# Attention and gated feed-forward on one core: long load runs, half-height projection tiles, ACT weight casts and an order from a list scheduler in the kernel

## The chip, the core and the metric

One NeuronCore of a Trainium2 chip. The metric is the device time of one execution in microseconds (us); "span" is the part of it that the trace shows, some 2 us less. PE is the matmul engine, DVE the vector engine, ACT the scalar engine, POOL the general one, SP the one that only issues transfers. In the traces of this case an engine that meets a wait lets nothing pass that stands behind it in its own order (ACT stood 4.3 us before a cast while an eviction was ready); the case turns on that.

## The reference, cut to what matters

```python
# q, k, v: (4, 4, 1088, 32) f32; S1, S2: (8, 32); w_gate, w_val: (128, 1536); w_out: (1536, 128)
a = einsum('rd,bhsd->bhsr', S1, x); b = einsum('rd,bhsd->bhsr', S2, x)   # for x = q and x = k
phi = outer(a, b).reshape(..., 64)
kv = einsum('bhsf,bhsd->bhfd', phi(k), v);  z = phi(k).sum(axis=2)
x = (phi(q) @ kv) / (phi(q) @ z + 1e-6)          # heads joined: (4352, 128)
out = (relu(x @ w_gate) * (x @ w_val)) @ w_out   # (4352, 128) f32
```

The attention part of a batch is small and serial; the feed-forward part is large and regular: nine chunks (eight of 512 tokens, one of 256) of 12 slots, each slot with a gate, a value and an output matmul on PE, a relu on ACT and a multiply on DVE.

## The kernel before

Loads go out in many pieces (k and q of a batch: six transfers each, in runs of 1 KB and 128 B), weights are cast to fp16 on the way in by POOL's transfers, and q, k come in two buffers that rotate.

```python
def load_kq(src, b, name, engs):
    dst = inp.tile([128, NBLK, D], FP32, name=name)          # bufs=2
    for h in range(H):
        engs[h % len(engs)].dma_start(
            out=dst[h * D:(h + 1) * D, 0:32].rearrange("t (g c) d -> t g (c d)", g=4),
            in_=src[b, h, 0:SM, :].rearrange("(g t c) d -> t g (c d)", g=4, t=32))
    ...
nc.gpsimd.dma_start(out=wg_sb, in_=moe_w_gate...)            # f32 -> f16 in the transfer
```

The projection contracts over all 128 rows (4 heads x 32) with a block-diagonal S, into 32-column tiles; the sums z are made by a 128x32 matmul after each pair of key-value matmuls:

```python
nc.tensor.matmul(ps[32*g:32*g+32, s*n:s*n+m], s_bd[:, s], kT[b][:, c_cols(g, c0, ...)], ...)
...
for p in range(2):
    nc.tensor.matmul(ps[:, p*64:(p+1)*64]..., st["kp", b, c][:, p*128:(p+1)*128], v4[b][:, 2*p:2*p+2, c], ...)
nc.tensor.matmul(ps[32*j:32*j+32, 128:160], ab[:, 0, o]..., ab[:, 1, o]..., ...)     # z
```

The order is written as a table of slots and then left to the compiler's scheduler (`MANUAL = False`). A chunk's output leaves in one transfer of 256 KB.

## Time and profile before

| | before |
|---|---|
| time, median of the runs | 152.24 us |
| span of the profiled run | 149.9 us |
| first gate matmul | 33.21 us |
| first gate matmul to last output eviction | 112.34 us |
| last output eviction to the end | 4.35 us |

The last three rows cut the span into start, steady stretch and tail. The start is read from the first g_ps record of PE, the end of the stretch from the end of ACT's last o_sb record. The lines themselves are in the prediction below.

### The profile page before, as it was taken

The page shows a single profiled execution, that of the slowest core. Times are in us where ns is not written, and L with a number is a line of the kernel's source. Part 1 is how long each engine was busy: PE and PEld are TensorE (multiplying, and loading weights), DVE is VectorE, ACT ScalarE, POOL GpSimd, SP SyncE. Part 2 cuts the span into 40 slices and gives each one's busy share as a digit, 9 for nine tenths or more (in the row PEclk, how much of TensorE's full clock was granted, in tenths as well). Part 3 has the DMA queues.
Part 4 walks back from the last instruction along what each step waited for, and adds up shares of the span by engine and source line. Part 5 has one row for each costly group of instructions (what it writes and reads, how often), then busy time and mean ns, then how long its engine had stood idle before and what let it go on. Part 6 is the DMA issues. An engine that isn't in the chain of part 4 may idle for free.

```text
span 149.9 us, 2886 instructions
## 1 busy us (share of the span) xinstructions
PE 120.5 (80%) x1038; PEld 61.7 (41%) x1038; DVE 100.2 (67%) x213; ACT 82.1 (55%) x146; POOL 51.5 (34%) x75
## 2 busy tenths in 40 slices
PE   0035966269999998799999879999998899999950
PEld 0014645144463443355544335554543353444620
DVE  4133754905968688698798685867788386889840
ACT  3000000057756557696467469855658785998940
POOL 7500981722820045575001763620176034000000
PEclk9999999758999999999999999999999999999996
DMA  4999999930000070005201000100010010010101
GB/s 80 201 221 200 134 214 205 185 79 2 4 0 0 4 210 0 2 0 171 63 0 70 2 4 0 70 0 4 0 70 0 4 56 16 0 70 7 69 1 37
DMA packets 13535, 9.20 MB, mean 61 GB/s; under 512 B 5840, under 2 KB 12240, under 8 KB 13520
## 3 DMA queue, kind: packets, MB, share of 16 engines
q1 hardware_dynamic: 8032, 6.62, 17.4%
q0 software_dynamic: 5040, 2.29, 13.1%
q10 hardware_dynamic: 448, 0.10, 0.4%
q8 instruction: 8, 0.13, 0.3%
q14 instruction: 7, 0.06, 0.1%
HBM read 9.08 MB, written 2.23 MB: 75 GB/s over the span
## 4 chain that ended last, share of the span: by engine, by line
PE 63%; POOL 9%; DVE 8%; DMA 6%; issue 4%; ACT 3%; SPq 2%; POOLq 1%; DVEq 0%; ACTq 0%
PE g_ps L375 14%; PE v_ps L379 13%; PE ot_ps L393 13%; POOL qp L217 7%; DMA k<-in_k_dram 6%; PE ps_a L285 6%; PE kv_ps L242 5%; DVE ht L386 4%; PE ps_a L337 3%; PE ps_a L201 3%; PE kv_ps L237 3%; POOL a L319 2%; PE ps_a L358 2%; ACT g_sb L377 2%; PE ps_a L407 1%
## 5 line engine op out<-in xcount | busy, mean ns | idle before, releaser
L386 DVE TENSOR_TENSOR ht<-g_sb,v_ps 128x512 f16<-128x512 f16 (+1 forms) x108 | 68.9, 652 | 25.2 <-ACT g_sb L377 15.5
L377 ACT ACTIVATE g_sb<-g_ps 128x512 f16<-128x512 f32 (+1 forms) x108 | 60.6, 576 | 28.9 <-PE g_ps L375 23.7
L379 PE MATMUL v_ps<-xT,wv_sb 128*128 128x512 f16 (+1 forms) x108 | 40.0, 371 | 0.4
L375 PE MATMUL g_ps<-xT,wg_sb 128*128 128x512 f16 (+1 forms) x108 | 39.9, 374 | 0.1
L393 PE MATMUL ot_ps<-ht,wo_sb 128*128 128x512 f16 (+1 forms) x108 | 38.5, 368 | 0.2 <-DVE ht L386 0.2
L217 POOL TENSOR_TENSOR kp<-kab 128x512 f16<-128x512 f32 (+1 forms) x18 | 17.2, 976 | 22.9 <-DVE kab L212 19.2
L343 ACT COPY qpt<-ps_a 128x1024 f16<-128x1024 f16 (+1 forms) x9 | 8.7, 963 | 27.9 <-PE ps_a L337 27.9
L217 POOL TENSOR_TENSOR qp<-a,qab 128x512 f16<-128x512 f32 (+2 forms) x18 | 18.3, 1037 | 0.5
L201 PE MATMUL ps_a<-kT,s_bd 128*32 128x128 f32 x128 | 7.2, 314 | 12.0 <-DVE s_bd L158 8.2
L337 PE MATMUL ps_a<-ident,qp 128*128 128x128 f16 (+1 forms) x72 | 9.6, 238 | 8.4 <-POOL qp L217 8.4
L302 POOL TENSOR_TENSOR bw<-qab 128x128 f32<-128x128 f32 (+1 forms) x8 | 3.6, 454 | 37.1 <-DVE qab L295 37.1
L379 PEld LDWEIGHTS <-wv_sb 128*128 128x128 f16 x108 | 10.6, 98 | 9.6 <-issue 3.4
L375 PEld LDWEIGHTS <-wg_sb 128*128 128x128 f16 x108 | 10.6, 98 | 8.6 <-issue 2.1
L393 PEld LDWEIGHTS <-wo_sb 128*128 128x128 f16 x108 | 10.2, 97 | 7.8 <-issue 1.7
L337 PEld LDWEIGHTS <-qp 128*128 128x128 f16 (+1 forms) x72 | 5.8, 107 | 17.2 <-POOL qp L217 13.5
L285 PE MATMUL ps_a<-qT,s_bd 128*32 128x128 f32 x128 | 9.8, 314 | 0.9 <-DVE qT L188 0.9
L201 PEld LDWEIGHTS ps_a<-kT,s_bd 128*32 128x32 f32 x128 | 3.8, 120 | 15.0 <-DVE s_bd L158 8.2
L242 PE MATMUL kv_ps<-kab 128*32 128x32 f32 x72 | 9.6, 218 | 0.0
L181 DVE STREAM_TRANSPOSE kT<-k 128x384 f32<-128x384 f32 (+1 forms) x12 | 6.3, 536 | 4.3 <-DMA k<-in_k_dram 4.3
L237 PE MATMUL kv_ps<-v,kp 128*128 128x64 f16 x72 | 8.8, 204 | 0.2 <-DVE kp L217 0.2
L237 PEld LDWEIGHTS <-kp 128*128 128x128 f16 x72 | 6.2, 101 | 5.9 <-DVE kp L217 0.3
L285 PEld LDWEIGHTS ps_a<-qT,s_bd 128*32 128x32 f32 x128 | 5.5, 121 | 5.6 <-issue 1.9
(63 smaller groups left out, 98.9 us busy)
## 6 DMA issues: line engine op xcount, KB each, us to landing
k<-in_k_dram SPq DMA_DIRECT2D x16, 128.0 KB
q<-in_q_dram SPq DMA_DIRECT2D x16, 128.0 KB
out_dram<-o_sb SPq DMA_DIRECT2D x8, 256.0 KB
v<-in_v_dram POOLq DMA_DIRECT2D x4, 256.0 KB, 6.3
wg_sb<-in_moe_w_gate_dram POOLq DMA_DIRECT2D x1, 384.0 KB, 7.7
wv_sb<-in_moe_w_val_dram POOLq DMA_DIRECT2D x1, 384.0 KB, 9.7
wo_sb<-in_moe_w_out_dram POOLq DMA_DIRECT2D x1, 384.0 KB, 14.1
k<-in_k_dram SPq DMA_DIRECT2D x8, 16.0 KB
```

Of the source, the lines that this page charges most:

```text
L201: nc.tensor.matmul(ps[32 * g:32 * g + 32, s * n:s * n + m], s_bd[:, s], kT[b][:, c_cols(g, c0, min(c1, NC))], start=True, stop=True)
L217: eng.tensor_tensor(out=dst.rearrange("p c (h i j) -> p (c h) i j", h=H, i=R), in0=a.rearrange("p c h i -> p (c h) i")[:, :, :, None].to_b ...
L237: nc.tensor.matmul(ps[:, p * 64:(p + 1) * 64].rearrange("p (h d) -> p h d", h=2), st["kp", b, c][:, p * 128:(p + 1) * 128], v4[b][:, 2 * p ...
L242: nc.tensor.matmul(ps[32 * j:32 * j + 32, 128:160], ab[:, 0, o].rearrange("p h r -> p (h r)"), ab[:, 1, o].rearrange("p h r -> p (h r)"), ...
L285: nc.tensor.matmul(ps[32 * g:32 * g + 32, s * 128:(s + 1) * 128], s_bd[:, s] if s < 2 else w_s[b], qT[b][:, c_cols(g, 4 * i, 4 * i + 4)], ...
L337: nc.tensor.transpose(st["qpt", key][:, p, c * n:(c + 1) * n], st["qp", key, c][0:n, p * 128:(p + 1) * 128], ident16[0:n, 0:n])
L343: nc.scalar.copy(out=t[:, :, 0:4 * n], in_=st["qpt", key][:, :, 0:4 * n])
L375: nc.tensor.matmul(g_ps[:, :cs], wg_sb[:, j], xT[:, c0:c0 + cs], start=True, stop=True)
L377: nc.scalar.activation(out=g_sb[:, :cs], in_=g_ps[:, :cs], func=ACTF.Relu)
L379: nc.tensor.matmul(v_ps[:, :cs], wv_sb[:, j], xT[:, c0:c0 + cs], start=True, stop=True)
L386: nc.vector.tensor_tensor(out=st["ht", i][:, j, :cs], in0=g_sb[:, :cs], in1=v_ps[:, :cs], op=ALU.mult)
L393: nc.tensor.matmul(st["ot", i][:, :cs], wo_sb[:, j], st["ht", i][:, j, :cs], start=(j == 0), stop=(j == NJ - 1))
```

## The change

Its intent: let k arrive first and in long runs, so that the feed-forward part starts early; halve the PE time of the projections with 64-row tiles, two of them one above the other, each pair writing its own PSUM bank; take z out from between the key-value matmuls; keep the casting of weights off the transfers; and fix the order of every engine by a list scheduler that runs while the kernel is built, with a cost per step and a table of the times at which loads land. The core of the diff:

```diff
-MANUAL = False
+MANUAL = True
+LAND = {"s": 4.8, "k": (5.0, 12.0, 15.0, 20.0), "q": (7.0, 13.0, 16.0, 21.0), "v": 8.0, "w": (11.0, 13.0, 15.0)}
...
+    k4 = [big.tile([128, NB * D], FP32, name=f"k4_{b}") for b in range(B)]
+    def load_kq(dst, src, b, after=None):
+        behind(after, nc.sync.dma_start(out=dst[b], in_=src[b].rearrange("h (t c) d -> (h t) (c d)", t=32)))
...
+        for rp in range(2):
+            for g in range(4):
+                nc.tensor.matmul(st["ps", key][rp][32 * g:32 * g + 32, lo:lo + 32 * n],
+                                 s_bd[64 * rp:64 * rp + 64].rearrange("p h r x -> p (h r x)"),
+                                 xt[64 * rp:64 * rp + 64, cols(g, c0, c0 + n)], start=True, stop=True)
...
-            nc.sync.dma_start(out=out[...].rearrange("(p c) m -> p c m", p=128)[:, 4 * hf:4 * hf + 4], in_=o)
+            for g0 in (0, 2):
+                ...
+                d = bass.AP(d.tensor, d.offset, [[w * DM, 2], d.ap[0], [1, 4 * DM]])
+                nc.sync.dma_start(out=d, in_=o[32 * g0:32 * g0 + 64].rearrange("p c m -> p (c m)"))
...
+    def cast_w(i):
+        nc.scalar.copy(out=(wg_sb, wv_sb, wo_sb)[i], in_=w_in[i])
...
+    order = run()
+    for _, s in order:
+        s[4](*s[5])
+        if s[4] == k_transpose and s[5] == (0, 1):
+            for i in range(2):
+                load_w(i, st["last"])
+        if s[4] == q_transpose and s[5][1] == 1 and s[5][0] + 1 < B:
+            load_kq(k4, k, s[5][0] + 1, st["last"])
+            if s[5][0] == 0:
+                load_w(2, None)
+            load_kq(q4, q, s[5][0] + 1)
```

## The prediction

> **What bounds the kernel now.** I read the page's busy shares and its 40 slices first, then the chain of work that ended last in order of time, the groups by shape, the waits and the timeline. The shares alone say "PE 80%", but they average a start with no feed-forward work and three steady stages, so I cut the span there.
>
> ```profile
> PE 120.5 (80%) x1038; PEld 61.7 (41%) x1038; DVE 100.2 (67%) x213; ACT 82.1 (55%) x146; POOL 51.5 (34%) x75
> PE   0035966269999998799999879999998899999950
> ACT  3000000057756557696467469855658785998940
> PEclk9999999758999999999999999999999999999996
> DMA  4999999930000070005201000100010010010101
> GB/s 80 201 221 200 134 214 205 185 79 2 4 0 0 4 210 0 2 0 171 63 0 70 2 4 0 70 0 4 0 70 0 4 56 16 0 70 7 69 1 37
> ```
>
> See that ACT, which has two passes in every feed-forward slot, does nothing for eight slices of 3.75 us: the first third of a slice past 30 us is pure start. In that time the DMA engines are full (9) but move only some 200 GB/s. The chain in time gives the start's steps and the stage length:
>
> ```profile
> 3.69 8.77 DMA k<-in_k_dram
> 12.55 0.52 DVE kT L181
> 13.12 1.08 PE ps_a L201 x11
> ...
> 21.85 3.12 PE ps_a L285 x48
> ...
> 30.46 1.02 ACT qpt L343
> 31.52 1.01 PE ps_a L358 x2
> ...
> 33.39 0.43 PE g_ps L375
> ...
> 35.36 0.57 PE ps_a L201 x16
> ...
> 63.33 0.57 PE ps_a L201 x16
> ...
> 91.30 0.57 PE ps_a L201 x16
> ```
>
> The first k piece is complete only at 12.5 us; from there a serial chain of 20.7 us leads to the first gate matmul (33.2 in the timeline). After that the same instruction of the next batch's k projection returns every 27.97 us: that is one stage, 24 feed-forward slots with one batch's attention hidden beside them. After the third (91.30 + 27.97 = 119.3) come 26.3 us to the last eviction (145.55) and 4.35 us of output DMA to 149.9. The reported time is 152.26, 2.4 over the span.
>
> Inside a stage, the PE row is 9s, and the windows 40 to 50, 70 to 80, 90 to 100 and 100 to 110 us each show PE busy 10.00 of 10. But a PE record's end is modelled (386 ns for a matmul that starts 0.216 us after its neighbour), so I count by start-to-start. One z matmul between key-value matmuls looks so:
>
> ```profile
> 69.97 0.22 PE L237 MATMUL kv_ps<-v,kp 128*128 128x64 f16 x2
> 70.12 0.25 PE L242 MATMUL kv_ps<-kab 128*32 128x32 f32 x2
> ```
>
> and the next instruction starts at 70.30: 0.33 us for four small matmuls. Per stage: feed-forward 72 x 0.216 = 15.6; output transposes 0.4; k projection 0.57 + 0.36 + 0.22 = 1.15 (chain); kv and z 9 x 0.33 = 3.0; q projections three times the 16 in 0.57 = 1.7; q transposes 16 x 0.06 = 1.0; numerator 4 x 0.22 = 0.9; the small z product 0.3. Sum 24.0 of 27.97, or 86%. DVE is not far behind: 24 multiplies at 0.62 start to start (pairs end in 1.25, single 0.68) = 14.9 plus some 5.5 of attention = 20.4. ACT: 24 x 0.55 plus 4.2 (two each of output cast, output scale and xT cast, less overlap) plus 2 of qpt evictions = 19. So in a stage PE is the bound, with DVE close, and 4 us is lost to order.
>
> **What the Trainium skill says.** "TensorEngine Tiling (Array Packing)", Key Properties: changing the tiling mode drains the array, different tiles run in parallel; its list of configurations gives 8 tiles for 64x32 and 4 for 128x32. The trace agrees on the drain: a 128x32 matmul behind a 512-column one starts 0.32 us after it (47.16 to 47.48), where a like-mode neighbour starts 0.22 after. Eight side by side no line of this trace shows yet. "DMA: Bandwidth & Descriptors", Measured: 64 KB 138 GB/s, 1 MB 341. The trace agrees on the low side: 13535 packets of mean 680 bytes, 12240 under 2 KB, about 200 GB/s with all engines full. "TensorE: Matmul & The Clock Gate", Part 1: a PE that was idle runs at half rate for about 3.4 us; here the first g_ps and v_ps start 0.4 apart, later ones 0.22, and PEclk shows 7 and 5 there. The start will pay this after the change too.
>
> **The change part by part.**
> 1. Loads. k and q of a batch become one transfer each with 4352-byte runs (batch 0's k two of 2176), weights come as fp32 behind k, every batch has its own buffer. Batch 0's k is 0.56 MB; alone at about 300 GB/s (an estimate between the 200 here and the skill's 341) that is 1.9 us plus about 2.5 of issue and latency: complete at 5 to 6 us in place of 12.5. Gain 6.5 to 7.
> 2. Weights. 2.36 MB, after k and beside q, v and the next k: 4.6 MB in all before the last one, 15 us at 300 GB/s, done near 17 to 18. Three ACT casts of 1536 columns, about 1.5 each by qpt's 1.01 for 1024. ACT is idle then, but they stand ahead of its first qpt eviction in an in-order queue: the one place where the start could be given back.
> 3. Chain from k to the first g. Now 20.7. New terms, from this trace's durations: transposes 0.7; k projection cold, half of 1.6 = 0.9; two evictions 0.9; outer products and q transposes on DVE 1.75 + 1.3 with z, zs, w_s in their shade = 3.3; q projection of 4 blocks cold 0.9 (before: 3.1, because both q pieces ran interleaved); eviction 0.65; bw, den, rden, a on DVE 1.2 (before 1.7 by way of POOL); outer product, three pieces on DVE 1.1 (before 2.6 on POOL and a 0.7 wait); transposes 0.4; qpt 1.0; numerator 0.5 (two half-height tiles side by side, before 1.0); xT 0.6; hops 1.3. Sum 13.5. First g at 5.8 + 13.5 = 19.3; I take 20. Gain 13.
> 4. PE work in a stage. k projection 1.15 to 0.6; z in one block of 18 instead of nine switches, 9 x 0.18 to 0.5; kv 9 x 0.15 to 1.0; q from 1.7 to 1.1 (the S1, S2 two thirds halve, w does not); numerator 0.9 to 0.5. 24.0 becomes 21.0.
> 5. DVE barely changes: fewer, wider transposes save some 0.4 a stage, and padding memsets go. DVE 20 a stage, nearly level with PE.
> 6. Order. The scheduler in the kernel sets each engine's order from costs near the start-to-start ones above. It can recover part of the 4 us of slack, not all: with PE 21, DVE 20, ACT 19 and two PSUM buffers for g and v, I take 91% of PE: 23.0 per stage. Gain 5 a stage, 15 in all.
> 7. End: 26.3 to 23.5 (the last batch's leftover q work no longer spread out, POOL's queue hop of 1.1 at 123.3 gone, feed-forward slots still 0.65 to 0.7); output DMA 4.4, unchanged in kind.
>
> Sum: 20 + 2 to the mark of the first k projection + 3 x 23.0 + 23.5 + 4.4 + 2.4 = 121.3 us.
>
> **The rivals.** (a) ACT is held by a late weight: if bandwidth stays at 210 GB/s, 4.6 MB end at 24 us and the first qpt waits for the third cast; the first g comes at 26 to 27, time 127 to 128. For it: these 200 GB/s with engines full. Against it: small packets explain that rate. (b) DVE becomes the bound: PE's saving of 3 us a stage is then hidden, stages stay near 25.5, time 128 to 129. For: 20 against 21, each multiply waits for two others. Against: DVE idles 25 us before its multiplies now, mostly for ACT g_sb, an order matter. (c) The fixed order is brittle: a mispredicted step blocks an in-order engine, stages 27 as now and only the start is gained: 137. Against: a cost list near measured pitches. (d) Better than thought: PE and DVE both at 95%, stages 21.5, last part 22, start 18.5: 114.
>
> **Range and chances.** The start's 11 to 15 us are the surest; even with (c) the kernel is 10% faster. Between (d) and (a) or (b) lies 114 to 129. I predict 121, range 114 to 130; faster by over 2% 0.97, within 2% 0.02, slower 0.01 (only if a load or the z block stalls every stage).
>
> **What would show it.** Step 1: the k transposes begin at 5 to 6.5 us and GB/s in the first slices passes 300. Step 2: the three casts end before the first qpt; if ACT's qpt starts directly behind a cast that waited for a DMA, rival (a). Step 3: first g_ps at 18.5 to 21.5. Step 4: z matmuls in one run of about 0.5, no 0.33 per block. Step 6: the k projections 22 to 24 apart; DVE idle before its multiplies well under 25 us. Wrong if PE has new idle in the stages while DVE is full, or POOL (13 us a stage with its DMA issues) holds the q transposes.

## The result, and the profile after

The changed kernel takes 137.24 us (median of 135.81 to 138.55); the ratio to the kernel before is 0.898 (0.890 to 0.906). Ratios here are the mean time of one kernel's fast runs over that of the other's fast runs of the same rounds, so not quite the ratio of the medians. It is faster by 10%, and outside the range of 114 to 130.

| us | before | predicted | after (profiled run, 137.69) |
|---|---|---|---|
| first gate matmul | 33.21 | 20.0 | 26.61 |
| stretch to the last output eviction | 112.34 | 94.5 | 100.21 |
| tail | 4.35 | 4.4 | 8.78 |
| outside the span (the profiled run before took 151.67) | 1.8 | 2.4 | 2.1 |

The predicted stretch is what its sum leaves: 121.3 - 20 - 4.4 - 2.4. The 2.4 outside the span is a slip: it sets one run's time, 152.26, against the span of another, of 151.67. All three parts inside the span came out long: 6.6, 5.7 and 4.4 us.

The page of the kernel after, shares and slices (40 slices, now of 3.39 us):

```profile
PE 104.1 (77%) x838; PEld 48.4 (36%) x838; DVE 95.6 (70%) x198; ACT 84.6 (62%) x149; POOL 50.7 (37%) x72
PE   0007774599999875999779999999999999999100
ACT  3000442677266775857838955997999999986200
DMA  4935996292635019100011010011011011010110
GB/s 127 220 73 145 357 302 224 28 99 78 252 47 60 0 21 333 43 35 0 6 37 41 6 46 30 2 30 48 0 34 46 7 39 36 25 49 15 47 40 18
```

Three things differ from the rows of the kernel before. The DMA row has a hole in the third slice (3, and 73 GB/s), at the very time when the kernel needs its loads. Later, GB/s reaches 357, so the long runs do move faster. And in the last two slices PE and ACT show 0 while 40 and 18 GB/s still pass: a tail. The chain of work that ended last, in order of time (start, duration, what), tells the start and one stop in the middle:

```profile
1.57 7.09 DMA xall<-in_S_dram
8.76 0.26 DVE y L157
9.43 0.67 DVE kT L175
10.14 1.84 PE ps_a L187 x16
...
15.26 7.58 DMA w_in<-in_moe_w_out_dram
22.86 1.47 ACT wo_sb L422
24.34 0.92 ACT qpt L354
...
26.61 0.59 PE g_ps L540
...
48.49 0.67 DVE qT L175
49.17 3.65 DMA k<-in_k_dram
52.98 0.53 issue
```

The start is not held by k at all: it is held by xall, the 32 KB of S1 and S2, because y, made from it, stands ahead of the k transposes in DVE's order. The DMA view up to 4.1 us shows that k, 0.56 MB at the head of SP's queue q1, has passed by then, while of S in ACT's queue q10 little more than half has:

```profile
q1 hardware_dynamic: 292, 0.57, 43.9%
q10 hardware_dynamic: 152, 0.02, 3.0%
```

In the packets of the kept trace the last one of k ends at 4.03 us, the last one of S at 8.04. Then comes w_out, whose cast stands ahead of the first qpt eviction in ACT's order. At 49.17 a load of k is issued behind a q transpose, and DVE stops for it.

### The profile page after: what moved, and what is told of

The parts are those of the page before. It is cut to its first block, busy times and chain, and to the rows that moved or that the text cites. A ratio compares the mean times of both kernels' runs of the same rounds, so it can differ in the third digit from the quotient of the medians.

```text
span 135.6 us, 2420 instructions
## 1 busy us (share of the span) xinstructions
PE 104.1 (77%) x838; PEld 48.4 (36%) x838; DVE 95.6 (70%) x198; ACT 84.6 (62%) x149; POOL 50.7 (37%) x72
## 4 chain that ended last, share of the span: by engine, by line
PE 58%; DMA 14%; DVE 11%; ACT 8%; issue 2%; ACTq 1%; SPq 0%; DVEq 0%
PE v_ps L551 15%; PE g_ps L540 15%; PE ot_ps L384 14%; DVE ht L556 6%; DMA w_in<-in_moe_w_out_dram 6%; DMA xall<-in_S_dram 5%; PE ps_a L187 5%; ACT g_sb L545 4%; DMA k<-in_k_dram 3%; PE ps_a L369 2%; PE ps_a L348 2%; DVE qT L175 1%; PE kv_ps L228 1%; PE ps_a L299 1%; PE ps_a L398 1%
## 5 line engine op out<-in xcount | busy, mean ns | idle before, releaser
L556 DVE TENSOR_TENSOR ht<-g_sb,v_ps 128x512 f16<-128x512 f16 (+1 forms) x108 | 66.5, 649 | 10.2 <-PE v_ps L551 3.3
L210 POOL TENSOR_TENSOR kp<-kab 128x512 f16<-128x512 f32 (+2 forms) x16 | 17.0, 1086 | 11.0 <-DVE kab L194 11.0
L187 PE MATMUL ps_a<-kT,s_bd 64*32 64x288 f32 x64 | 4.7, 549 | 10.1 <-DVE kT L175 10.1
L315 POOL TENSOR_TENSOR bw<-qab,qw 128x256 f32<-128x256 f32 (+2 forms) x5 | 3.3, 655 | 21.1 <-DVE qw L306 21.1
L228 PEld LDWEIGHTS <-kp 128*128 128x128 f16 (+1 forms) x72 | 6.0, 105 | 9.6 <-issue 4.2
L93 POOL DMA_DIRECT2D v<-in_v_dram x16 | 9.0, 568 | 0.1
L228 PE MATMUL kv_ps<-v,kp 128*128 128x64 f16 (+1 forms) x72 | 8.0, 205 | 0.9 <-DVE kp L210 0.9
L175 DVE STREAM_TRANSPOSE kT<-k 128x544 f32<-128x544 f32 x8 | 5.5, 718 | 2.8 <-DMA k<-in_k_dram 2.8
L175 DVE STREAM_TRANSPOSE qT<-q 128x544 f32<-128x544 f32 x8 | 5.8, 724 | 2.3 <-DMA q<-in_q_dram 2.3
L373 ACT CAST xT<-ps_a 128x512 f16<-128x512 f32 (+1 forms) x9 | 5.3, 588 | 1.1 <-PE ps_a L369 0.7
```

The source lines that it names most:

```text
L93: nc.gpsimd.dma_start(out=v4[b][32 * g:32 * g + 32, :, 0:n].rearrange("p h c d -> p h (c d)"), in_=x[:, :, CB[g] * D:(CB[g] + n) * D],)
L175: st["last"] = nc.vector.transpose(out=dst[:, a:e], in_=src[:, a:e])
L187: nc.tensor.matmul(st["ps", key][rp][32 * g:32 * g + 32, lo:lo + 32 * n], s_bd[64 * rp:64 * rp + 64].rearrange("p h r x -> p (h r x)"), xt ...
L210: eng.tensor_tensor(out=dst, in0=a[:, :, :, None].to_broadcast([np, n, R, R]), in1=bb[:, :, None, :].to_broadcast([np, n, R, R]), op=ALU.mult)
L228: i = nc.tensor.matmul(ps[:, p].rearrange("p (h d) -> p h d", h=2), st["kp", b, c][0:np, p * 128:(p + 1) * 128], v4[b][0:np, 2 * p:2 * p + ...
L556: nc.vector.tensor_tensor(out=st["ht", i][:, j, :cs], in0=st["gs", n][:, :cs], in1=st["v", n][:, :cs], op=ALU.mult)
```

## The experiments

Four theories compete for the 16 us. **Landing times:** loads land later than the table says and an in-order engine stands in front of each. **Tail:** the new output pattern is slow. **Engine limit:** PE (or DVE) simply has more work in a stage than I counted. **Order:** the list scheduler's order is worse than I gave it credit for. All runs below gave correct results. Times are medians of four runs; the highest run of the kernel after (138.55), of e6 (136.06) and of e7 (134.11) was counted as slow, all others as fast. Gains and ratios use fast runs alone, so the kernel after counts as 136.78 below. Its fast runs lie between 135.81 and 137.69, so a gain under some 2 us is not clear of the spread in time, and there the cut of the profiled run must speak. The stretch is steadier: 100.21 to 100.50 in the four kernels (after, e1 to e3) whose edits do not aim at it. The kernel before took 152.5 to 152.8 beside them; e9 to e12 ran on another chip than e1 to e8, and it took 152.72 beside e8 and 152.76 beside them.

| run | time | first gate matmul | stretch | tail |
|---|---|---|---|---|
| after | 136.78 (all four: 137.24) | 26.61 | 100.21 | 8.78 |
| e1 S first | 135.23 | 23.01 | 100.25 | 8.84 |
| e2 output patterns | 131.33 | 25.23 | 100.50 | 4.07 |
| e3 w_out early | 135.87 | 24.27 | 100.34 | 8.99 |
| e4 k, q early | 135.28 | 24.83 | 98.21 | 8.86 |
| e7 true table only | 132.00 (all four: 132.18) | 24.29 | 97.44 | 8.87 |
| e8 e1 to e4 together | 127.89 | 23.31 | 98.32 | 4.07 |
| e5 e8, 128-row tiles | 130.90 | 24.88 | 100.05 | 4.07 |
| e6 e8, compiler's order | 132.71 (all four: 133.21) | 30.17 | 95.92 | 4.11 |
| e12 e8, true table | 123.74 | 22.59 | 94.89 | 4.12 |

(The last three columns are of the profiled run of each.)

### e1: the small S load ahead of k

```diff
-        nc.scalar.dma_start(out=xall[:, i], in_=sm[None].to_broadcast([16, R, D]))
+        nc.sync.dma_start(out=xall[:, i], in_=sm[None].to_broadcast([16, R, D]))
```

> Only edit to the changed kernel: the two small S1/S2 loads are issued by SP ahead of k, instead of by ACT beside it. Theory (the start is held by the S load: y waits for it until 8.76 us, and in DVE's order the k transposes and through them the weight loads stand behind y): y starts at 4 to 5.5 us, the k transposes when k lands (6 to 7), first gate matmul 2 to 4 us earlier (26.6 to about 23.5), time 137.2 to about 134. Rival (k itself lands only at 8 to 9 us, so the S load is no loss): first gate matmul within 1 us of 26.6, time 136.5 to 138.

135.23 us, first gate matmul at 23.01. The timeline of DVE in this run (in brackets, how long the engine was idle before it, and on what):

```profile
4.90 0.25 DVE L157 STREAM_TRANSPOSE y<-xall 128x64 f32<-128x64 f32 x1 [3.17 <-DMA xall<-in_S_dram]
5.49 0.74 DVE L175 STREAM_TRANSPOSE kT<-k 128x544 f32<-128x544 f32 x1
7.08 0.74 DVE L175 STREAM_TRANSPOSE kT<-k 128x544 f32<-128x544 f32 x1 [0.84 <-DMA k<-in_k_dram]
```

y starts at 4.90 in place of 8.76, and now DVE waits for k itself, whose second half is there at 7.08. So the theory holds in the trace: the S load cost the start. That k is later than in the kernel after is the price of this edit: SP issues it behind S, at 2.19 in place of 0.81, and its last packet ends at 6.69 in place of 4.03. The time fell by 1.6, which is within the spread, and not by 3. The S load lands at different times from run to run (y at 8.76 in the profiled run of the kernel after, at 8.31 in e7, at 7.5 to 7.8 in e2 to e4, all with the same loads up to there), so that run of the kernel after was a late one, and up to 1.2 us of an earlier first gate matmul in e2 to e4 is not their edit's. Beside the S load, k, q and v move at that time. "DMA: Bandwidth & Descriptors", Queues, rings and completion order, says that each DMA engine takes turns between the queues packet by packet. In the kernel after, the 256 packets of 128 B of S take 0.01 us each but are spread from 2.68 to 8.04 us, among packets of k and q of 2176 and 4352 B (0.11 and 0.21 us each) and of v; in e1, at the head of SP's queue, the same packets pass between 2.29 and 4.31. Turns between the queues would fit; but a packet of that page holds several descriptors, the records here are single rows, and which engine took which is not on record, so the turns themselves are not shown.

### e2: output transfers that start with 32 rows in place of 2

```diff
-            for g0 in (0, 2):                      # pattern [[w*DM, 2], [34*DM, 32], [1, 512]]
-                nc.sync.dma_start(out=d, in_=o[32 * g0:32 * g0 + 64]...)
+            for g in range(4):                     # pattern [[34*DM, 32], [1, 512]]
+                nc.sync.dma_start(out=x[:, c:c + 4].rearrange("t c m -> t (c m)"),
+                                  in_=o[32 * g:32 * g + 32].rearrange("p c m -> p (c m)"))
```

(and the last chunk's four transfers split in the same way into eight)

> Only edit: each output transfer whose DRAM pattern starts with a dimension of 2 is split into one of 32 rows per group (4 instead of 2 for a chunk, 8 instead of 4 at the end). Theory (a leading dimension of 2 keeps a transfer on 2 of the 16 DMA engines; 51 GB/s flat in the tail is 2/16 of the 385 GB/s of the kernel before): from the last o_sb eviction to the end 4.0 to 5.5 us instead of 8.8, time 137.2 to about 133; nothing else moves. Rival (the tail is the cost of many small rows and of issue): still 8 us or more from the last eviction to the end, time 136.5 to 138.5.

131.33 us, a gain of 5.5 us. The tail is 4.07, so 4.7 us are the tail's. The profiled run also starts earlier (25.23 for 26.61), but that is not the edit's: S happened to land 1.2 us sooner. GB/s in the DMA view, 40 slices each, of before (140 to 150 us), after (120 to 136) and e2 (118 to 130), in this order, each of its own kernel:

```profile
GB/s 0 0 0 0 0 0 57 385 385 221 0 0 0 0 0 0 0 0 0 0 0 0 0 0 0 0 0 115 123 53 119 113 2 0 0 0 0 0 33 0
```

```profile
GB/s 51 51 51 51 51 31 0 0 0 20 15 15 26 41 51 46 31 51 51 51 51 41 31 36 26 46 47 42 44 44 44 44 41 29 19 0 0 0 0 0
```

```profile
GB/s 0 0 0 0 0 0 0 0 0 0 0 0 0 0 143 103 184 103 123 191 27 0 0 0 0 0 0 0 60 50 108 38 74 101 9 0 0 0 0 0
```

Before, a chunk's 256 KB passes at up to 385 GB/s. After, the same bytes pass at a flat 51, about 2/16 of 385, and the last chunk's transfers stand behind them until the end of the span. "DMA: Bandwidth & Descriptors", Why a DMA increments its semaphore by 16 and not by 1 (the paragraph on how many engines), says that a transfer runs on the largest number of engines, up to 16, that divides the slowest dimension of both patterns. In the change that dimension is 2. The trace agrees: the packets of 2048 B keep 2.1 engines busy on average between 120 and 122 us, and 16 between 141.75 and 142.25 us of the kernel before, at 0.08 to 0.09 us each in both. And 32 in its place brings the tail back. This could have been read from the diff.

### e3: w_out issued with the other weights

```diff
-            for i in range(2):
+            for i in range(3):
                 load_w(i, st["last"])
...
-            if s[5][0] == 0:
-                load_w(2, None)
```

> Only edit: the load of w_out is issued directly behind those of w_gate and w_val, before the next k. Theory (ACT's in-order queue waits 4.3 us for it ahead of the first qpt eviction): its cast ends by 20.5 us, first qpt at about 22, first gate matmul at 24 to 24.8 instead of 26.6, time 137.2 to about 135. Rival (the first gate matmul is set by POOL's and PE's transposes or the feed-forward in stage one is limited by the crammed attention work anyway): the first gate matmul moves but the time stays within 0.7 us of 137.2.

135.87 us, 0.9 less, within the spread; ACT's wait for w_out fell from 4.3 to 1.1 us, the first gate matmul came at 24.27. Against e2, whose S load landed within 0.2 us of this run's, that is 1.0 us earlier. So the rival (a) of the prediction, "ACT is held by a late weight", is true, and worth a little over 1 us of the start. It is not worth all of the 2.3 us by which the cast held the eviction, because the next wait stands right behind it: in e3's chain POOL's three outer products of the second half of q (21.77 to 24.03) and PE's transposes of them, ahead of the first gate matmul in PE's order, lead to it. This is what the rival of this experiment named, and what the prediction named as a sign of being wrong ("POOL ... holds the q transposes"). But its reason there was a low bandwidth. The weights run at up to 446 GB/s in slices of the DMA view between 12 and 16 us of the kernel after; w_out was late because it was issued at 15.26, behind a q transpose.

### e4: k and q of batches 2 and 3 loaded at once

```diff
-        if s[4] == q_transpose and s[5][1] == 1 and s[5][0] + 1 < B:
-            load_kq(k4, k, s[5][0] + 1, st["last"])
+        if s[4] == q_transpose and s[5] == (0, 1):
+            load_kq(k4, k, 1, st["last"])
...
+            for b in range(2, B):
+                load_kq(k4, k, b)
+                load_kq(q4, q, b)
```

> Only edit: k and q of batches 2 and 3 are loaded at once behind those of batch 1, instead of each behind the last q transpose of the batch before. Theory (DVE's order holds a k transpose that waits for its load for 2.5 us at 50.3, and ACT and PE stop with it): that wait is gone, time 137.2 to 134.5 or 135. Rival (the wait falls in slack, or the early transfers delay w_out and with it the first gate matmul): time 136.5 to 139.

135.28 us, a gain of 1.5. DVE's wait for k at 52.8 us is gone and the stretch shrinks from 100.21 to 98.21, clear of its spread; the theory holds with the size expected, of the stretch (the time itself is just above the 134.5 to 135 expected). The gate on the q transpose, meant to keep the DMA engines free for what is needed sooner, let batch 3's k be issued at 49.17 when the table told the scheduler that it would be there at 20.

### e7: only the table of landing times corrected

```diff
-LAND = {"s": 4.8, "k": (5.0, 12.0, 15.0, 20.0), "q": (7.0, 13.0, 16.0, 21.0), "v": 8.0, "w": (11.0, 13.0, 15.0)}
+LAND = {"s": 8.7, "k": (8.7, 21.0, 36.0, 53.0), "q": (9.0, 25.7, 37.0, 54.0), "v": 9.5, "w": (15.2, 17.0, 22.8)}
```

> Only edit to the changed kernel: the table of landing times that the scheduler in the kernel takes is set to what its trace shows (S 8.7, k 8.7, 21, 36, 53, q 9, 25.7, 37, 54, weights 15.2, 17, 22.8 us) in place of (S 4.8, k 5, 12, 15, 20, q 7, 13, 16, 21, weights 11, 13, 15). Theory (wrong landing times made in-order engines stand at late loads): first qpt goes ahead of the w_out cast, first gate matmul at 23.5 to 25 in place of 26.6, no DVE wait for k of over 1 us, time 137.2 to 133 or 135. Rival (only earlier loads help; the order is near free): time within 1 us of 137.2.

The loads are the same and in the same queues; the scheduler only has other landing times (v's too, 9.5 for 8.0, which the expectation leaves out). 132.00 us: 4.8 us for thirteen numbers. The first gate matmul is at 24.29, the stretch 97.44. The timeline of ACT and PE in this run shows the first step of it:

```profile
21.91 1.01 ACT L354 COPY qpt<-ps_a 128x1024 f16<-128x1024 f16 x1 [3.88 <-PE ps_a L348]
...
24.29 0.58 PE L540 MATMUL g_ps<-xT,wg_sb 128*128 128x512 f16 x1 [0.67 <-ACT xT L373]
...
25.40 1.46 ACT L422 CAST wo_sb<-w_in 128x1536 f16<-128x1536 f32 x1
```

The eviction goes ahead of the cast of w_out, and no engine waits for k or q any more. So the table matters, and by more than any wait for a load in the stretch. But it is not a test of the order alone: the later loads are issued behind transposes, so with the order the times of issue moved too. SP's timeline shows it for w_out, first in the kernel after, then in e7:

```profile
15.26 0.43 SPq L110 DMA_DIRECT2D w_in<-in_moe_w_out_dram  x1
```

```profile
11.91 0.60 SPq L110 DMA_DIRECT2D w_in<-in_moe_w_out_dram  x1
```

Batch 3's k goes out at 45.48 in place of 49.17. In e7 the last packet of w_out ends at 19.94, before the eviction at 21.91, so the cast could hardly have held it. How much of the 4.8 us comes from the order and how much from the earlier loads, this run does not show.

### e8: the four edits e1 to e4 together

> All four edits at once (S loads first on SP, output transfers on 32-row patterns, w_out and every later k and q loaded early). Theory (start, tail and the k wait are separate terms and add up): first gate matmul at 20 to 21.5 us, tail 4.1 us, from first gate matmul to last eviction 98.2 us as with the early k and q alone, time 124 to 126. Rival (one fix uncovers another wait, as the loads now queue together): first gate matmul later than 22 or a stretch over 99, time 127 to 130.

127.89 us, ratio 0.839 (0.834 to 0.844). Tail and stretch came as expected (4.07 and 98.3), the start did not: 23.31, as the rival said. Singly the four gained 1.6, 5.5, 0.9 and 1.5, together 8.9 of 9.4, so as times they nearly add up. In this run the second half of k is there only at 8.01 (7.08 in e1; 7.91 to 8.65 in e9 to e12, with the same loads up to there), and the chain from there to the first gate matmul is 15.3 us, where the prediction had 13.5. The first eviction of qpt, at 20.04, now waits for PE's transposes and no longer for a weight, and the chain to the first gate matmul runs, as in e3, over POOL's outer products (20.81 to 23.08): a term uncovered behind the one removed.

### e5: e8 with the 64-row tiles undone

```diff
-                                 s_bd[64 * rp:64 * rp + 64].rearrange("p h r x -> p (h r x)"),
-                                 xt[64 * rp:64 * rp + 64, cols(g, c0, c0 + n)], start=True, stop=True)
+                                 s_f[:, rp],                    # 128 rows, zero outside the pair's 64
+                                 xt[:, cols(g, c0, c0 + n)], start=True, stop=True)
```

> All four edits, and the 64-row tiles undone: the two head pairs are projected with all 128 rows and a zero-padded weight, so four tiles side by side in place of eight, same results, same order. Theory (PE has slack in the steady stages, so halving the projections bought little): the projection block of a k batch is 0.3 to 0.6 us longer on PE, and the time rises by 0 to 1.5 us. Rival (PE sets the stages, as the prediction said): 0.5 us for k and 0.5 for q of each batch on the path, time up by 2.5 to 4 us.

130.90 us, 3.0 more than e8. PE's timeline, the k projection of a later batch, first in e8, then in e5:

```profile
61.38 0.72 PE L187 MATMUL ps_a<-kT,s_bd 64*32 64x288 f32 x16
```

```profile
64.08 1.18 PE L192 MATMUL ps_a<-kT,s_f 128*32 128x288 f32 x16
```

The half-height tiles do run side by side: 0.46 us less for a k batch, and 0.41 (1.07 to 0.66) for a q batch. This answers what the skill's list of tile configurations left open in the prediction. The stretch grew by 1.7 us; of the 1.6 us at the start some 0.7 is a later k (8.75 against 8.01), which is not the tile's. So the part is worth between 2 and 3 us, nearer to the rival (2.5 to 4) than to my theory (0 to 1.5). No run takes back the long load runs, the casts on ACT or the block of z, so what each of these is worth is not shown.

### e6: e8 with the compiler's order

```diff
-MANUAL = True
+MANUAL = False
```

> All four edits, and the order on the engines left to the compiler's scheduler as in the kernel before, in place of the list scheduler in the kernel. Theory (the fixed order is a real part of the gain of the steady stages): stretch from first gate matmul to last eviction grows from 98 to 103 or more, time up by 4 us or more. Rival (the order buys nothing once work is removed): time within 2 us of the run with all four edits.

132.71 us, 4.8 more than e8. But my expectation was wrong in its place: the stretch is 95.92, shorter than 98.32. The order of the list scheduler gains at the start (first gate matmul at 23.31 in place of 30.17) and not in the stages; part of that is a shift, since work of later batches that e6 did before its late first gate matmul need not be done after it. In e6 the k projection waits until 12.84, because DVE made s_bd from y only after two k and four q transposes. So the order is worth 5 us, all of it net in the start. (The steps are still handed to the compiler in the list scheduler's sequence, by the code; what part that plays is not shown.)

### e9, e10, e11: a little more work on one engine in every slot

Each repeats part of an operation on e8, with the same result and order: PE the first half of the value matmul, DVE 64 columns of the multiply, ACT 64 columns of the relu.

```diff
+        nc.tensor.matmul(st["v", n][:, :cs // 2], wv_sb[:, j], xT[:, c0:c0 + cs // 2], start=True, stop=True)   # e9
+        nc.vector.tensor_tensor(out=st["ht", i][:, j, :64], in0=st["gs", n][:, :64], in1=st["v", n][:, :64], op=ALU.mult)   # e10
+        nc.scalar.activation(out=st["gs", n][:, :64], in_=st["g", n][:, :64], func=ACTF.Relu)   # e11
```

> All four edits, and PE does the first half of every value matmul twice (same result, same order): 0.108 us more per slot, 11.0 us in all. Theory now (no engine sets the steady stages alone; the g and v buffers pass the slot round PE, ACT and DVE): time up by 4 to 8 us on 127.9. If PE sets the stages as the prediction said: up by 9 to 11. If PE has slack: up by less than 3.

> All four edits, and DVE multiplies the first 64 columns of every slot twice: some 0.13 us more per slot (64 columns at the slope of the two ht forms plus a start), about 14 us in all. If DVE sets the stages (rival b of the prediction): time up by 12 to 15 us on 127.9. Theory now (shared): up by 7 to 11. If PE sets them: up by less than 5.

> All four edits, and ACT does relu on the first 64 columns of every slot twice: some 0.13 to 0.2 us more per slot, 14 to 20 us in all. Theory now: up by 3 to 8 us on 127.9, most of it in the last stages, where ACT is 9 tenths busy; if ACT has slack, less than 3; if it sets the stages, 12 or more.

The added work on DVE and ACT was larger than I had estimated. From the timeline of DVE in e10, where DVE runs without a pause:

```profile
112.19 0.21 DVE L555 TENSOR_TENSOR ht<-g_sb,v_ps 128x64 f16<-128x64 f16 x1
112.43 0.69 DVE L557 TENSOR_TENSOR ht<-g_sb,v_ps 128x512 f16<-128x512 f16 x1
```

the 64 columns occupy 0.24 us from start to start, and on ACT in e11 0.25 (112.15 to 112.40). So the sums added are 11.0 us on PE (96 x 0.108 and 12 x 0.054, by the 0.216 per 512 columns), 108 x 0.24 = 25.9 on DVE and 108 x 0.25 = 27.0 on ACT.

| | added | time | more than e8 | share that shows |
|---|---|---|---|---|
| e9 PE | 11.0 | 135.56 | 7.7 | 0.70 |
| e10 DVE | 25.9 | 143.81 | 15.9 | 0.61 |
| e11 ACT | 27.0 | 140.62 | 12.7 | 0.47 |

No engine has a share near 1 and none near 0. By the letter of my expectations, 15.9 and 12.7 would make DVE and ACT each the one that sets the stages; they were set for additions of 14 and 14 to 20 us, so I read the shares in their place. PE comes first, as the prediction said, but all three set the stages together: the additions to DVE and ACT are large enough to shift the balance, so their shares are of that size of step, not of the first microsecond.

### e12: e8 with the table corrected for it

```diff
+LAND = {"s": 4.9, "k": (7.9, 20.0, 24.0, 27.0), "q": (9.0, 22.0, 25.5, 28.5), "v": 9.5, "w": (13.1, 15.1, 17.7)}
```

> All four edits, and the scheduler's table of landing times set to what the trace of the run with all four edits shows (S 4.9, k 7.9, 20, 24, 27, q 9, 22, 25.5, 28.5, v 9.5, weights 13.1, 15.1, 17.7 us). Theory (correcting the table alone was worth 5 us, of which the early loads already hold most): time 125.5 to 127.5. Rival (with the loads early the table no longer matters): within 0.7 us of 127.9.

123.74 us (123.45 to 123.86), better than I had expected, ratio to the kernel before 0.810 (0.805 to 0.816). It beats both kernels: 13.0 us under the change. From its page:

```profile
span 121.6 us, 2457 instructions
PE 103.1 (85%) x838; PEld 48.1 (40%) x838; DVE 95.1 (78%) x198; ACT 83.3 (69%) x149; POOL 51.0 (42%) x72
PE   0055965799998999999999999999999999999930
GB/s 7 236 226 263 383 351 409 412 201 89 30 10 17 43 43 5 3 0 3 73 13 5 86 0 5 21 68 0 0 86 0 8 86 0 3 84 0 67 29 34
```

Set beside the rows of the kernel after: the DMA engines move without a hole from the second slice on, at over 400 GB/s when the weights and later batches pass, PE works almost without a break, and the same busy time of PE (103 us, 104 after) is now 85% of the span. The stretch is 94.89, where the prediction had 94.5: with loads early and known to the scheduler, its length is what was predicted. It is not a wait for a load that went, for e8 has none: its last one, of 0.7 us for q, ends at 22.14, before the first gate matmul. The true table gave the scheduler another order, and why that one is 3.4 us better no run shows. A table that is wrong in another way was not tried, so a lucky shuffle of the order is not excluded, though both corrected tables (e7, e12) gained.

## Why the prediction was wrong

The direction was right. The part held to be "the surest", 11 to 15 us from the start, gained 6.6. By its own steps:

1. **Loads.** "complete at 5 to 6 us in place of 12.5" held for k, whose last packet ends at 4.03, and the rate passed 300 GB/s (336 to 425 in slices of 0.1 us between 2.7 and 3.6 us). What failed is the step from the landing to the transposes: nobody could take k before 8.8, because y stands ahead of them in DVE's order and waits for S. I looked at the large loads only; the wait for xall was in the profile before as well (4.0 us of DVE). The k transposes began at 9.35, the second at some 10.0, so this step cost 4.2 us of the 6.6. (The 12.5 was misread too: it is the last k piece of the kernel before; DVE took the first two at 7.48 and 8.08.)
2. **Weights.** "done near 17 to 18" is the step that failed for w_out. The cast was sized right (1.47 us; "about 1.5"), the bandwidth was better than assumed, but I reckoned bytes over a rate from the start on and did not follow the gates in the diff: w_out is issued at 15.26 and lands at 22.84. PE's transposes ended at 21.95 and the eviction behind the cast began at 24.24: the other 2.3 to 2.4 us of the 6.6, of which e3 got back little over 1, since POOL's outer products stood next in line. Rival (a) had the mechanism and the time of the first gate matmul ("26 to 27"), for another reason.
3. **Chain.** 13.5 us (by its own terms 13.1: half of 1.6 is 0.8, and 1.75 + 1.3 is 3.05), of which the rounding to 20 made 14.2, was a little low: 16.6 in the kernel after with the 2.3 of the cast in it, 14.7 to 15.3 in e12 and e8. The mis-sized terms are the two first projections, put at 0.9 each: in e8 that of k took 1.21 after its second transpose (8.81 to 10.02, with 14 of its 16 records), and in the kernel after that of q took 1.26 (15.99 to 17.25). The 1.84 that the chain after shows for k has the wait for the second k transpose in it. That the first matmuls of the feed-forward would run slowly was right: they stand 0.43 us apart up to 31.4 us and 0.22 from 33.1 on, though the PEclk row shows 9 there.
4. **PE work.** Right, and too small if anything. The z block takes 0.44 to 0.45 in the chain ("0.5"), the k projection 0.65 (at 66.64; "0.6"). A key-value pair beside feed-forward matmuls now takes 0.06 from start to start, as PE's timeline of the kernel after shows, where I left 0.11:

```profile
55.36 0.22 PE L228 MATMUL kv_ps<-v,kp 128*128 128x64 f16 x2
55.42 0.38 PE L384 MATMUL ot_ps<-ht,wo_sb 128*128 128x512 f16 x1
```

So more than half of the 0.15 that such a pair took before belonged to the change of tile shape between it and z. The kernel before shows it too, at 71.52 us, where no z follows the pair: 0.06 to the next instruction.

5. **DVE.** Right in kind, and too small: 95.6 us busy for 100.2 before, where step 5 saved some 0.4 a stage.
6. **Order.** "I take 91% of PE: 23.0 per stage": this is the step that failed in the stretch. 100.21 us came in place of 94.5. The equal stages that it counts did not come about: the k projections start at 10.14, 29.04, 38.31 and 66.58 us, so 18.9, 9.3 and 28.3 apart and not "22 to 24". The scheduler put the attention of the later batches beside the first 48 slots; by the starts of their multiplies these took 56 us, and the next 48, which have little of it, 36. All that e4, e8 and e12 gain in the stretch lies in those first 48. Of the 5.7 us, loading k and q early gave back 2.0 (e4), which is a wait at a late load; the table alone gave 2.8 (e7), and the two together with the other edits left 94.89 (e12). It was not that PE has more work (its busy time is the same in e12), nor that an order of that kind cannot reach it. But e6 says that, at equal loads and with the uncorrected table, this order did nothing for the stages that the compiler's does not do. What I called a recovery of slack came only with the corrected table; by what step, beyond the wait for k, stays open.
7. **Tail.** "output DMA 4.4, unchanged in kind" failed: 8.78, for the leading dimension of 2 (e2). I had read the pattern in the diff and not what the skill's page says of it.

Summed: 121.3 predicted, + 4.2 (S) + 2.4 (w_out) + 5.7 (stretch) + 4.4 (tail) - 0.3 (outside the span) = 137.7; the profiled run took 137.69. Rival (c), "stages 27 as now and only the start is gained: 137", hit the time by accident: the start gained 6.6, the stretch 12.1, and the tail gave 4.4 back. Its mechanism, a mispredicted step that blocks an in-order engine, is there, at the casts (4.3 us of ACT) and at q and k (2.3 and 2.5 us of DVE). (One reading that did no harm: ACT's row has seven slices of 0, not eight.)

What stays open: whether the S load was slow for its queue or for its place, since e1 moved it to another queue and to the front at once; by what step the true table shortens the stretch, and how much of e12's gain over e8 belongs to which number of it.

## What to carry to other kernels

An order that a scheduler fixes at build time is only as good as its landing times: an in-order engine that meets one late load stops everything behind it, so read the real landings from the trace, put them in, and repeat after each change of the loads. Where loads are issued behind steps of that order, a new order moves the loads as well, so look at both before you credit either. Follow the small loads and the issue gates as carefully as the large transfers, and look at the slowest dimension of every transfer pattern. Cut a prediction into start, stretch and tail, since each failed here for its own reason.

## What the Trainium skill lacked or had wrong

- "DMA: Bandwidth & Descriptors" has no time for a small load beside large ones: 32 KB in a queue of its own landed 7.1 us after its issue in the kernel after, and was used at 4.9 us, not 8.8, when it went first in the large loads' queue.
- "TensorEngine Tiling (Array Packing)", Key Properties: the drain at a change of mode is stated without a cost. A pair of 64-column matmuls took 0.15 us beside a 128x32 one and 0.06 without. Eight 64x32 tiles in place of four of 128x32 took 0.72 us in place of 1.18 for the same columns: 1.6 times as a whole block, within the twofold that the page gives as the most.
